# Attention in sessions of two tiles over four PSUM banks, with the products on the other four

## The chip, the cores and the metric

The kernel runs on one core of a Trainium2 chip. The metric is the device time of one execution in microseconds. An executed kernel is also profiled once; that execution has its own time and its own span from first to last instruction, and the rows below come from it. The engines are TensorE (PE, with its weight loads as PEld), VectorE (DVE), ScalarE (ACT), GpSimd (POOL) and SyncE (SP), which issues the DMAs here. Each works its instructions off in the order of the program, and waits for others by semaphores.

## The reference

Batch 8, 8 heads, 576 positions, head size 64, all float32. Three parts follow one another:

```python
# 1. attention inside chunks of 64 positions
scores = scale * np.matmul(q_c, k_c.transpose(0, 1, 2, 4, 3))
scores = scores - np.max(scores, axis=-1, keepdims=True)
attn = np.exp(scores)
attn = attn / (np.sum(attn, axis=-1, keepdims=True) + 1e-09)
out = np.matmul(attn, v_c)
# 2. x is out as (8, 576, 512); layer norm, then a feed-forward of width 2048
mu = np.mean(x, axis=-1, keepdims=True)
var = np.mean((x - mu) ** 2, axis=-1, keepdims=True)
xn = (x - mu) / np.sqrt(var + 1e-06) * g_ln
x = x + np.maximum(xn @ w_ch1, 0.0) @ w_ch2
# 3. h = relu(x @ w_in), width 1024; a convolution of 3 taps along the sequence,
#    a sigmoid gate on its sum, and out = (h * gate) @ w_out
```

## The kernel before

There are 4608 rows of 512, taken as 36 tiles of 128 rows; four tiles make a slab, so there are nine slabs. The change lies in the first stage, which computes attention, the layer norm and the product with `w_ch1`. The later stages (the product with `w_ch2`, the convolution, the last product) are untouched.

The steps of a tile T are methods of `Attention`, each with a letter: `L` loads q, k and v; `S` multiplies q and k (16 small matmuls of 64x64, each of two passes); `M` takes the maximum of each row on VectorE; `E` takes exponentials on ScalarE, in eight instructions of 64 columns, four to a half, and their sums; `R` the reciprocal of the sums; `P` transposes the exponentials on TensorE and `C` copies them out of PSUM on ScalarE; `V` multiplies them with v; `X` scales by the reciprocals on VectorE and stores; `B` and `x` are the layer norm; `T` transposes the normed rows and `e` copies them to `bst`, the slab's input.

PSUM has eight banks. `S` and `V` of a tile use one half each of a pair of banks: banks 0 and 1. `P` goes to bank 0, `T` to bank 3.

The product with `w_ch1` multiplies matrices of 2x2 blocks by seven products in place of eight. Of each slab four groups G are computed, each of seven products n = 1 to 7; each product is 12 matmuls of 256 columns (each operand is split into a high and a low part, three matmuls per product of parts, lines 113 to 115). Products 1, 6, 7 and 4 of a group add up in one bank, 4 or 5 by the group's parity, and after each ScalarE copies the sum out as u1, u6, u7, u4 (lines 605 and 614). Products 5 and 3 add up in another, 6 or 7 by parity: VectorE adds 5 to u7 once product 7 is there, and the sum of 5 and 3 to u6. Product 2 goes to bank 2, and VectorE adds it to u1. These adds are line 159, called from `product`. The results are stored by SP to `hd`.

The order is written out by hand. Time is counted in slots, one product each: slot t = 28p + 7G + s, with s the place in the tuple `SLOTS`; its second number is the lag: a product with lag 1 belongs to the group before. Attention runs one slab ahead of the products. `session(t, tv)` hangs steps of two tiles behind the products of slots t to t + 4: V of tile tv with S, M of tile tv + 1 at t, E in two halves at t + 1 and t + 2, B and x of tv there too, and R, P, C of tv + 1 with T, e of tv at t + 4. In the steady stage a session begins every seven slots. In the last group of a slab each product is also followed by the preparation of the next slab's operand (`Slab.both`: a cast on ScalarE, a subtraction on VectorE, and the block sums `j` that they need).

In slab 0 the first slots also carry the rest of the conversion of `w_ch1` from its 64-bit input: the steps with letters a, t, m, n, g, h, l and s in `START`, behind the bar, one line for each slot; a, g, h are on ScalarE, t, m, n, l, s on VectorE.

Of the kernel before, what the change touches and what calls it, by code (L numbers as in the profile page):

```python
# [23 lines left out]
h7 B2 e1 B3 h6 u1 l7 v1 y3 l8 z3 s4 e3 y2 s6 z2 s5 e2 l6 h11 j0 u2 j1 u3  # L24
s7 u5 v3 u7 h10 l11 j2 l10 u6 v2 h12 v6 j3 l12 u4 v5 h13 v4 l13 v7
|
S4 M4 E4 a8 t8 a10 t10 m8 n8
/ g8 a9 t9 m10 n10
/ g10 a11 a12 t11 t12 m9 R4 P4
/ C4 a14 n9 t14 g9 m12  # L30
/ h14 n12 m11 g12 n11 a13
/ l14 t13 g11 m14 h15
/ n14 s8 g14 l15 a15
/ h16 t15 s9 m13 l16 n13
/ s10 g13 s11 h21 h17
# [9 lines left out]
def attn_moe_moe2(  # L45
# [296 lines left out]
    class Attention:  # L342
# [13 lines left out]
        def tile(self, shape, tag, bufs):  # L356
            return self.p.tile(shape, F32, tag=tag, bufs=bufs, name=tag)

        def L(self, T):
            for nm, to in (("q", self.q), ("k", self.k)):  # L360
                t = self.tile([128, HP * 2 * 64], "r" + nm, 2)
                if T < N0:
                    src = (q0 if nm == "q" else k0)[T].rearrange("c d e j s -> e d c (j s)")
                    for e in range(2):
                        nc.sync.dma_start(
                            out=t[half(e)].rearrange("p (c n) -> p c n", c=2), in_=src[e]
                        )
                    to[T] = t.rearrange("p (c j s) -> p j c s", c=2, s=64)
                else:
                    src = (q if nm == "q" else k)[T - N0]  # L370
                    nc.sync.dma_start(out=t, in_=src.rearrange("e p j c s -> (e p) (j c s)"))
                    to[T] = t.rearrange("p (j c s) -> p j c s", c=2, s=64)
            t = self.tile([128, HP * 2 * 64], "rv", 3)
            nc.sync.dma_start(out=t, in_=v[T].rearrange("e s j c d -> (e s) (j c d)"))
            self.v[T] = t.rearrange("p (j c d) -> p j c d", c=2, d=64)
# [22 lines left out]

        def E(self, T, js=range(4)):
            if T not in self.pp:  # L400
                self.sm[T] = self.tile([128, 2, HP], "sm", 3)
                self.pp[T] = self.tile([128, HP, 2, 64], "pp", 2)
            sm, pp, mx = self.sm[T], self.pp[T], self.mx[T]
            for j in js:
                for e in range(2):
                    nc.scalar.activation(  # L406
                        out=pp[:, j, e, :], in_=self.both[T][:, e, j, :], func=AF.Exp, scale=SCALE,
                        bias=mx[:, e, j:j + 1], accum_out=sm[:, e, j:j + 1],
                    )
# [108 lines left out]
    with tc.manual_schedule():  # L518
# [20 lines left out]
        def one(step):  # L539
            kind, i = step[0], int(step[1:])  # L540
            if kind in "atmng":
                getattr(blocks[i // 4], kind)(i % 4)
            elif kind == "W":
                blocks[i // 4].W(i % 4, nc.sync)
            elif kind == "w":
                blocks[i // 4].W(i % 4, nc.scalar)
            elif kind == "s":
                blocks[i // 4].s(i % 4)
            elif kind in "hl":
                getattr(blocks[i // 7], kind)(i % 7)  # L550
            elif kind in "juv":
                getattr(slabs[0], kind)(i)
            elif kind == "S":
                at.S(i, (4, 6, 0, 4, 0)[i])
            elif kind == "V":
                at.V(i, (4, 6, 0, 4)[i])
            elif kind == "P":
                at.P(i, 0 if i > 3 else 2)
            elif kind in "y":
                at.x(i)  # L560
            elif kind == "z":
                at.T(i)
            else:
                getattr(at, kind)(i)
# [14 lines left out]
        def product(p, G, n):  # L579


            to = {1: 4 + G % 2, 6: 4 + G % 2, 7: 4 + G % 2, 4: 4 + G % 2, 5: 6 + G % 2, 3: 6 + G % 2, 2: 2}[n]
            x = slabs[p].xc[n]
            for i in range(2):
                f = 2 * G + i
                o = f % 4 * 128
                for kk in range(2):
                    w = wc[n, f // 4, kk]
                    mm3(bank[to][:, i * 256:(i + 1) * 256], w[:, 0, o:o + 128], w[:, 1, o:o + 128],
                        x[:, 0, kk], x[:, 1, kk], n in (1, 2, 5) and not i and not kk, kk == 1,  # L590
                        skip_group_check=True)

            def top(name):
                return su_p.tile([128, 2, 256], F32, tag=name, bufs=2, name=name)

            def flat(t):
                return t.rearrange("p a n -> p (a n)")

            def store(blk, t):
                nc.sync.dma_start(out=hd[p][G][:, blk], in_=t)  # L600

            if n in (1, 6, 7):

                t = tops[p, G, n] = top(f"u{n}")
                nc.scalar.copy(flat(t), bank[to])  # L605
            if n == 7:

                t = tops.pop((p, G, 7))
                plus(flat(t), bank[6 + G % 2], flat(t))
                store(3, t)  # L610
            if n == 4:

                t = top("u4")
                nc.scalar.copy(flat(t), bank[to])
                store(2, t)
            if n == 2:

                t = tops.pop((p, G, 1))
                plus(flat(t), bank[to], flat(t))
                store(0, t)  # L620
            if n == 3:

                t = tops.pop((p, G, 6))
                plus(flat(t), bank[to], flat(t))
                store(1, t)

        SLOTS = ((1, 0), (5, 0), (4, 1), (6, 0), (3, 1), (2, 0), (7, 0))
        events = {}

        def on(t, fn):  # L630
            events.setdefault(t, []).append(fn)

        def session(t, tv):

            ts = tv + 1 if tv + 1 < NTILE else None

            def begin():
                at.V(tv)
                if ts is not None:
                    at.S(ts)  # L640
                    at.M(ts)
                at.X(tv)
                if tv + 2 < NTILE:
                    at.L(tv + 2)

            on(t, begin)
            if ts is not None:
                on(t + 1, lambda: at.E(ts, (0, 1)))
                on(t + 2, lambda: at.E(ts, (2, 3)))
            on(t + 1, lambda: at.B(tv))  # L650
            on(t + 2, lambda: at.x(tv))

            if tv % 4 == 3:
                on(t + 3, lambda: (at.T(tv), at.e(tv)))
            if ts is not None:
                on(t + 4, lambda: (at.R(ts), at.P(ts)))
            if tv % 4 != 3:
                on(t + 4, lambda: at.T(tv))
            if ts is not None:
                on(t + 4, lambda: at.C(ts))  # L660
            if tv % 4 != 3:
                on(t + 4, lambda: at.e(tv))

        for tv in range(4, NTILE):

            t = 28 * (tv // 4 - 1) + 7 * (tv % 4 - 1) + 1
            session({4: 5, 5: 9, 6: 13, 7: 17}.get(tv, t), tv)

        class Down:

# [341 lines left out]
```

## Time and profile before

| | |
|---|---|
| Time, median of three runs | 1308.42 us (1308.25 to 1308.7) |
| Profiled execution: time, span | 1309.48 us, 1307.5 us |
| TensorE busy, of the span | 1249.2 us, 96% |
| VectorE busy | 748.9 us, 57% |
| ScalarE busy | 614.8 us, 47% |
| Mean granted clock of TensorE | 0.973 of full speed |
| First product of slab 0 starts | 45.1 us |
| First session of the steady stage (tile 8) starts | 118.0 us |
| A slab of the steady stage, between its sessions | 47.0 us |

A row of the timeline gives the start, the duration, the engine, the source line and operation, what is written and read, and how many instructions stand in it; a bracket at its end is the time that the engine was idle before it and who ended that. Matmuls overlap, so the distance between two starts is what one costs, not its duration. A row of the windows gives the busy time of every engine in a stretch.

### The profile page before, as it was taken

What the parts mean: (1) busy time and instruction counts of PE and PEld (TensorE: products, weight loads), DVE (VectorE), ACT (ScalarE), POOL (GpSimd) and SP (SyncE); (2) the same over time, 40 slices, a digit from 0 to 9 for tenths busy, and PEclk for the clock granted to TensorE, in tenths of its full rate; (3) what the DMA queues carried; (4) which work ended last, traced back from release to release, by engine and by line L of the source; (5) the groups of instructions that cost most, each with busy time, mean ns of one, the idle gap of its engine ahead of it and who ended that gap; (6) DMA issues with size and microseconds to landing.
All of it is one profiled execution on the core that took longest, in us unless ns stands there. A gap on an engine that the chain in (4) does not pass through costs nothing.

```text
span 1307.5 us, 23314 instructions
## 1 busy us (share of the span) xinstructions
PE 1249.2 (96%) x9096; PEld 1087.0 (83%) x9096; DVE 748.9 (57%) x1430; ACT 614.8 (47%) x1510; POOL 76.2 (6%) x172
## 2 busy tenths in 40 slices
PE   5559999999999989999999999999999999999998
PEld 4459999999999978787788888888788888888887
DVE  7986565566556557667733443343876655565540
ACT  6765555556556435343322222222765555455541
POOL 0000000000000000000000000000121211111100
PEclk6689999999999989999999999999999999999999
DMA  9534555555455358486444355432111111101001
GB/s 267 169 106 170 186 172 168 188 186 177 168 183 191 114 205 298 146 296 211 145 153 161 128 178 178 161 130 81 33 57 58 43 37 57 57 28 53 25 25 49
DMA packets 127021, 177.70 MB, mean 136 GB/s; under 512 B 12736, under 2 KB 72128, under 8 KB 126912
## 3 DMA queue, kind: packets, MB, share of 16 engines
q1 hardware_dynamic: 126912, 176.22, 40.3%
q8 instruction: 71, 1.16, 0.4%
q14 instruction: 38, 0.31, 0.1%
HBM read 110.13 MB, written 66.06 MB: 135 GB/s over the span
## 4 chain that ended last, share of the span: by engine, by line
PE 85%; DVE 6%; ACT 4%; DMA 3%; issue 1%; SPq 1%; POOL 0%; DVEq 0%; ACTq 0%; POOLq 0%
PE banks L113 27%; PE banks L114 26%; PE banks L115 26%; PE banks L380 3%; PE banks L462 1%; PE banks L420 1%; DMA w<-in_moe_w_ch_dram 1%; DVE w L156 1%; ACT pp L406 1%; DMA wd<-in_moe_w_ch_dram 1%; DVE w L151 0%; DMA x2d<-x2T 0%; ACT w L335 0%; DVE xr L159 0%; DVE w L145 0%
## 5 line engine op out<-in xcount | busy, mean ns | idle before, releaser
L113 PE MATMUL banks<-xc,w 128*128 128x256 f32 x1008 | 290.4, 288 | 7.6 <-ACT u L605 7.1
L114 PE MATMUL banks<-xc,w 128*128 128x256 f32 x1008 | 283.2, 281 | 4.5 <-DVE xc L156 4.5
L115 PE MATMUL banks<-xc,w 128*128 128x256 f32 x1008 | 282.9, 281 | 0.0
L685 ACT ACTIVATE hh<-hr 128x512 fp32r<-128x512 f32 x144 | 91.1, 632 | 262.0 <-PE banks L115 261.8
L686 DVE SCALAR_TENSOR_TENSOR hl<-hr,hh 128x512 fp32r<-128x512 f32 x144 | 99.2, 690 | 192.1 <-ACT hh L685 189.9
L113 PEld LDWEIGHTS banks<-xc,w 128*128 128x128 f32 x1008 | 193.3, 192 | 10.5 <-ACT u L605 7.5
L114 PEld LDWEIGHTS banks<-xc,w 128*128 128x128 f32 x1008 | 193.6, 192 | 4.7 <-DVE xc L156 4.7
L115 PEld LDWEIGHTS banks<-xc,w 128*128 128x128 f32 x1008 | 193.3, 192 | 0.0
L113 PE MATMUL banks<-w,hl 128*128 128x512 f32 x396 | 154.7, 391 | 0.0
L114 PE MATMUL banks<-w,hh 128*128 128x512 f32 x396 | 154.1, 389 | 0.0
L115 PE MATMUL banks<-w,hh 128*128 128x512 f32 x396 | 154.1, 389 | 0.0
L896 DVE SCALAR_TENSOR_TENSOR cv<-hb,cw_sb,cv 128x510 f32<-128x510 f32 (+31 forms) x256 | 117.2, 512 | 0.6
L113 PE MATMUL banks<-xb,w 128*128 128x512 f32 x288 | 113.5, 394 | 1.8 <-ACT hb L881 1.4
L114 PE MATMUL banks<-xb,w 128*128 128x512 f32 x288 | 113.0, 393 | 0.0
L115 PE MATMUL banks<-xb,w 128*128 128x512 f32 x288 | 112.9, 392 | 0.0
L159 DVE TENSOR_TENSOR u<-banks,u 128x512 f32<-128x512 f32 x108 | 73.6, 688 | 56.2 <-ACT u L605 31.1
L406 ACT ACTIVATE pp<-banks,mx 128x64 f32<-128x64 f32 x288 | 87.8, 336 | 8.1 <-DVE mx L397 5.4
L605 ACT COPY u<-banks 128x512 f32<-128x512 f32 x108 | 64.0, 593 | 56.7 <-PE banks L115 54.1
L113 PEld LDWEIGHTS banks<-w,hl 128*128 128x128 f32 x396 | 74.3, 188 | 17.4 <-DVE hl L686 2.1
L115 PEld LDWEIGHTS banks<-w,hh 128*128 128x128 f32 x396 | 74.3, 188 | 15.6
L114 PEld LDWEIGHTS banks<-w,hh 128*128 128x128 f32 x396 | 74.3, 188 | 15.2
L883 POOL COPY hal<-hb 128x2 f32<-128x2 f32 x64 | 41.8, 652 | 736.6 <-ACT hb L881 736.6
(106 smaller groups left out, 2197.8 us busy)
## 6 DMA issues: line engine op xcount, KB each, us to landing
hd<-u SPq DMA_DIRECT2D x144, 256.0 KB, 2.9
hr<-hd SPq DMA_DIRECT2D x72, 512.0 KB, 3.8
w<-in_moe_w_ch_dram SPq DMA_DIRECT2D x27, 512.0 KB, 6.8
rv<-in_v_dram SPq DMA_DIRECT2D x36, 256.0 KB, 3.7
xd<-x SPq DMA_DIRECT2D x36, 256.0 KB, 2.0
xr<-xd SPq DMA_DIRECT2D x36, 256.0 KB, 4.3
x2d<-x2T SPq DMA_DIRECT2D x36, 256.0 KB, 2.0
x2r<-x2d SPq DMA_DIRECT2D x36, 256.0 KB, 4.0
```

The lines of the kernel that those rows point to most:

```text
L113: nc.tensor.matmul(ps, ll, rh, start=first, stop=False, **kw)
L114: nc.tensor.matmul(ps, lh, rl, start=False, stop=False, **kw)
L115: nc.tensor.matmul(ps, lh, rh, start=False, stop=last, **kw)
L156: nc.vector.tensor_tensor(out=out, in0=a, in1=b, op=ALU.subtract)
L159: nc.vector.tensor_tensor(out=out, in0=a, in1=b, op=ALU.add)
L380: nc.tensor.matmul(ps[half(c), e, j, :], lt[half(e), j, c, :], rt[half(e), j, c, :], start=True, stop=True,)
L406: nc.scalar.activation(out=pp[:, j, e, :], in_=self.both[T][:, e, j, :], func=AF.Exp, scale=SCALE, bias=mx[:, e, j:j + 1], accum_out=sm[:, ...
L605: nc.scalar.copy(flat(t), bank[to])
L685: nc.scalar.activation(out=self.hh, in_=t, func=AF.Relu)
L686: nc.vector.scalar_tensor_tensor(out=self.hl, in0=t, scalar=0.0, in1=self.hh.bitcast(F32), op0=ALU.max, op1=ALU.subtract,)
L883: nc.gpsimd.tensor_copy(out=hal[:, f, :], in_=hb[:, 512:514])
L896: nc.vector.scalar_tensor_tensor(out=cv[:, a:e], in0=hb[:, a + tap:e + tap], scalar=cw_sb[:, tap, f:f + 1], in1=cv[:, a:e], op0=ALU.mult, ...
```

## The change

Sessions take two tiles in place of one: V of both, then S of the next two, and at their end P of both and T of both. The even tile of a pair uses banks 0 and 1, the odd one 2 and 3. Two sessions make a slab: they begin at its slots 0 and 13, and the step with P, T, e and C, now called `turn`, comes six slots later. The products are left with banks 4 to 7: 1, 6, 7, 4 stay on 4 and 5 by parity, 5 and 3 of every group use bank 6, 2 uses bank 7. The order of products in a group is 1, 2, 3 (of the group before), 6, 4 (of the group before), 5, 7, where it was 1, 5, 4, 6, 3, 2, 7. Loads of v are separate (`Lv`), and the early slots are rearranged: S4 and S5 both stand in slot 0, and tiles 4 and 5 begin at slot 7, tiles 6 and 7 at slot 14 (before: tiles 4 to 7 at slots 5, 9, 13 and 17).

```diff
-S4 M4 E4 a8 t8 a10 t10 m8 n8
-/ g8 a9 t9 m10 n10
-/ g10 a11 a12 t11 t12 m9 R4 P4
-/ C4 a14 n9 t14 g9 m12
-/ h14 n12 m11 g12 n11 a13
-/ l14 t13 g11 m14 h15
+S4 S5 M4 M5 E4 L6 L7 a8 t8 a10 t10 m8 n8
+/ E5 g8 a9 t9 m10 n10
+/ g10 a11 a12 t11 t12 m9
+/ a14 n9 t14 g9 m12
+/ R4 P4 C4 h14 n12 m11 g12 n11 a13
+/ R5 P5 C5 l14 t13 g11 m14 h15
...
-            to = {1: 4 + G % 2, 6: 4 + G % 2, 7: 4 + G % 2, 4: 4 + G % 2, 5: 6 + G % 2, 3: 6 + G % 2, 2: 2}[n]
+            to = {1: 4 + G % 2, 6: 4 + G % 2, 7: 4 + G % 2, 4: 4 + G % 2, 5: 6, 3: 6, 2: 7}[n]
...
-                plus(flat(t), bank[6 + G % 2], flat(t))
+                plus(flat(t), bank[6], flat(t))
...
-        SLOTS = ((1, 0), (5, 0), (4, 1), (6, 0), (3, 1), (2, 0), (7, 0))
+        SLOTS = ((1, 0), (2, 0), (3, 1), (6, 0), (4, 1), (5, 0), (7, 0))
...
+            tvs = tv, tv + 1
+            tss = [T for T in (tv + 2, tv + 3) if T < NTILE]
+            side = lambda T: T % 2 * 2
 
             def begin():
-                at.V(tv)
-                if ts is not None:
-                    at.S(ts)
-                    at.M(ts)
-                at.X(tv)
-                if tv + 2 < NTILE:
-                    at.L(tv + 2)
+                for T in tvs:
+                    at.V(T, side(T))
+                for T in tss:
+                    at.S(T, side(T))
+                for i in range(2):
+                    if tss:
+                        at.M(tss[i])
+                    at.X(tvs[i])
+                for T in tss:
+                    if T + 2 < NTILE:
+                        at.L(T + 2, late=True)
+                for T in tss:
+                    at.Lv(T)
+
+            def turn():
+                for T in tss:
+                    at.R(T)
+                    at.P(T, side(T))
+                for T in tvs:
+                    at.T(T, side(T) + 1)
+                for i in range(2):
+                    at.e(tvs[i])
+                    if tss:
+                        at.C(tss[i])
...
+            for i, T in enumerate(tss):
+                on(t + 1 + 2 * i, lambda T=T: at.E(T, (0, 1)))
+                on(t + 2 + 2 * i, lambda T=T: at.E(T, (2, 3)))
+            for i, T in enumerate(tvs):
+                on(t + 1 + i, lambda T=T: at.B(T))
+                on(t + 3 + i, lambda T=T: at.x(T))
+            on(t + 6, turn)
+
+        for tv in range(4, NTILE, 2):
+
+            t = 28 * (tv // 4 - 1) + (13 if tv % 4 else 0)
+            session({4: 7, 6: 14}.get(tv, t), tv)
```

The first place is TensorE at the start of a session in the steady stage, before the change: `rv,pt` is V, `rk,rq` is S, the rows around it are products.

```order
L114 MATMUL banks<-xc,w_1120 128x256
L115 MATMUL banks<-xc,w_1120 128x256
L380 MATMUL banks<-rv,pt 64x64 x16
L380 MATMUL banks<-rk,rq 64x64 x16
L113 MATMUL banks<-xc,w_363 128x256
L114 MATMUL banks<-xc,w_363 128x256
```

After the change the same place, where line 380 has become line 384, reads:

```order
L114 MATMUL banks<-xc,w_620 128x256
L115 MATMUL banks<-xc,w_620 128x256
L384 MATMUL banks<-rv,pt 64x64 x32
L384 MATMUL banks<-rk,rq 64x64 x32
L113 MATMUL banks<-xc,w_340 128x256
L114 MATMUL banks<-xc,w_340 128x256
```

Both tiles of a pair stand together, and the place occurs half as often.

The second place is VectorE in the last group of a slab. Before the change, from the add behind product 7 (`u_2135`) on, it has a J (`t`), a second, a subtraction for the next operand (`xc`), a third J, a second subtraction and the M and X of a session:

```order
L159 TENSOR_TENSOR u_2135<-banks,u_2135 128x512
L156 TENSOR_TENSOR t_2153<-bst 128x512
L156 TENSOR_TENSOR bst<-bst 128x2x256
L156 TENSOR_TENSOR xc<-bst,xc 128x512
L159 TENSOR_TENSOR bst<-bst 128x2x256
L156 TENSOR_TENSOR xc<-t_2153,xc 128x512
L396 TENSOR_REDUCE mx<-banks 128x8
L397 TENSOR_SCALAR mx<-mx 128x8
L434 TENSOR_TENSOR x<-banks,sm 128x2x4x64
```

After it, the same stretch from the add behind product 7 (`u_2180`) on, with the add to u1 (`u_2196`) and the add to u6 (`u_2107`), which is the last reader of bank 6 before product 5:

```order
L159 TENSOR_TENSOR u_2180<-banks,u_2180 128x512
L156 TENSOR_TENSOR t_2198<-bst 128x512
L156 TENSOR_TENSOR bst<-bst 128x2x256
L156 TENSOR_TENSOR xc<-bst,xc 128x512
L159 TENSOR_TENSOR bst<-bst 128x2x256
L159 TENSOR_TENSOR u_2196<-banks,u_2196 128x512
L156 TENSOR_TENSOR xc<-bst,xc 128x512
L156 TENSOR_TENSOR bst<-bst 128x2x256
L159 TENSOR_TENSOR u_2107<-banks,u_2107 128x512
L156 TENSOR_TENSOR xc<-bst,xc 128x512
```

The session has left the last group, and the adds of products 2 and 3 have moved forward, between the sums for the next slab.

## Rows read from the trace of the kernel before

**Rows 1.** The page, part 1: busy us, share of the span, instructions.

```profile
PE 1249.2 (96%) x9096; PEld 1087.0 (83%) x9096; DVE 748.9 (57%) x1430; ACT 614.8 (47%) x1510; POOL 76.2 (6%) x172
```

**Rows 2.** Windows: stretch, length, busy us and instructions per engine, clock, DMA.

```profile
60.00:84.00 24.00, 15.28 (x211) 14.30 (x210) 19.78 (x42) 17.07 (x42) 0.86 (x1) 0.78 0.25 78
84.00:112.00 28.00, 21.16 (x259) 20.08 (x259) 20.43 (x42) 15.03 (x55) 1.63 (x2) 0.84 0.35 114
213.00:260.00 47.00, 47.00 (x632) 46.15 (x634) 27.97 (x60) 26.59 (x96) 2.20 (x4) 1.00 0.54 180
```

**Rows 3.** Timeline of TensorE at V and S of a steady session.

```profile
164.59 0.28 PE L114 MATMUL banks<-xc,w 128*128 128x256 f32 x1
164.70 0.28 PE L115 MATMUL banks<-xc,w 128*128 128x256 f32 x1
164.91 0.69 PE L380 MATMUL banks<-rv,pt 64*64 64x64 f32 x32
165.43 0.65 PE L380 MATMUL banks<-rk,rq 64*64 64x64 f32 x32
166.00 0.38 PE L113 MATMUL banks<-xc,w 128*128 128x256 f32 x1
166.22 0.29 PE L114 MATMUL banks<-xc,w 128*128 128x256 f32 x1
```

**Rows 4.** Timeline of TensorE at P and T of that session.

```profile
171.45 0.28 PE L115 MATMUL banks<-xc,w 128*128 128x256 f32 x1
171.60 0.66 PE L420 MATMUL banks<-ident,pp 128*128 128x128 f32 x4
172.09 0.60 PE L462 MATMUL banks<-ident,xn 128*128 128x128 f32 x4
172.45 0.36 PE L113 MATMUL banks<-xc,w 128*128 128x256 f32 x1
172.65 0.28 PE L114 MATMUL banks<-xc,w 128*128 128x256 f32 x1
```

**Rows 5.** Timelines of VectorE and ScalarE there: the pace of each queue.

```profile
166.18 0.68 DVE L156 TENSOR_TENSOR xc<-t,xc 128x512 fp32r<-128x512 f32 x1
166.78 0.68 DVE L396 TENSOR_REDUCE mx<-banks 128x8 f32<-128x512 f32 x1
167.58 0.68 DVE L434 TENSOR_TENSOR x<-banks,sm 128x512 f32<-128x512 f32 x1
...
168.35 0.32 ACT L406 ACTIVATE pp<-banks,mx 128x64 f32<-128x64 f32 x1
...
169.53 0.60 ACT L605 COPY u<-banks 128x512 f32<-128x512 f32 x1
170.00 0.65 ACT L502 CAST xc<-bst 128x512 fp32r<-128x512 f32 x1
```

**Rows 6.** Timeline of TensorE, early stage: waits, and the first steady session.

```profile
53.63 0.58 PE L114 MATMUL banks<-xc,w 128*128 128x256 f32 x1 [4.46 <-DVE xc L156]
58.51 1.11 PE L420 MATMUL banks<-ident,pp 128*128 128x128 f32 x4 [2.17 <-ACT pp L406]
76.06 1.11 PE L420 MATMUL banks<-ident,pp 128*128 128x128 f32 x4 [3.94 <-ACT pp L406]
81.07 1.13 PE L380 MATMUL banks<-rv,pt 64*64 64x64 f32 x32 [3.04 <-ACT pt L426]
97.69 1.13 PE L380 MATMUL banks<-rv,pt 64*64 64x64 f32 x32 [5.74 <-ACT pt L426]
118.00 0.69 PE L380 MATMUL banks<-rv,pt 64*64 64x64 f32 x32
```

**Rows 7.** SP's issue of tile 5's k, and the landing of k loads there.

```profile
48.11 1.42 SPq L365 DMA_DIRECT2D rk<-in_k_dram  x2
...
DMA to landing us min/median/max: 6.3/7.2/8.2
```

**Rows 8.** TensorE's waits from 455 to 480 us: total, times, longest.

```profile
PE banks L113 <- ACT u L605: 6.5, 1, 6.5
```

More of the change, by code (lines that the diff above doesn't have):

```diff
@@ L357, in tile, with L @@
             return self.p.tile(shape, F32, tag=tag, bufs=bufs, name=tag)
-        def L(self, T):
+        def L(self, T, late=False):
             for nm, to in (("q", self.q), ("k", self.k)):
@@ L372, in L, with Lv @@
                     to[T] = t.rearrange("p (j c s) -> p j c s", c=2, s=64)
+            if not late:
+                self.Lv(T)
+        def Lv(self, T):
             t = self.tile([128, HP * 2 * 64], "rv", 3)
@@ L400, in E @@
             if T not in self.pp:
-                self.sm[T] = self.tile([128, 2, HP], "sm", 3)
+                self.sm[T] = self.tile([128, 2, HP], "sm", 4)
                 self.pp[T] = self.tile([128, HP, 2, 64], "pp", 2)
@@ L553, in one @@
             elif kind == "S":
-                at.S(i, (4, 6, 0, 4, 0)[i])
+                at.S(i, (4, 6, 0, 4, 0, 2)[i])
             elif kind == "V":
@@ L557, in one @@
             elif kind == "P":
-                at.P(i, 0 if i > 3 else 2)
+                at.P(i, i % 2 * 2 if i > 3 else 2)
+            elif kind == "L":
+                at.L(i, late=i > 5)
             elif kind in "y":
@@ L633, in session @@
         def session(t, tv):
-            ts = tv + 1 if tv + 1 < NTILE else None
+            tvs = tv, tv + 1
+            tss = [T for T in (tv + 2, tv + 3) if T < NTILE]
+            side = lambda T: T % 2 * 2
             def begin():
-                at.V(tv)
-                if ts is not None:
-                    at.S(ts)
-                    at.M(ts)
-                at.X(tv)
-                if tv + 2 < NTILE:
-                    at.L(tv + 2)
-            on(t, begin)
-            if ts is not None:
-                on(t + 1, lambda: at.E(ts, (0, 1)))
-                on(t + 2, lambda: at.E(ts, (2, 3)))
@@ L650, in session @@
[L650 to L667, printed above, removed]
+                for T in tvs:
+                    at.V(T, side(T))
```

## Prediction

> **What bounds the kernel now.** I read the page's list of engines first: TensorE is busy 96% of the span [rows 1], so what counts is what it does beside the products, and what makes it wait. The windows part the attention stage in two. From 60 to 112 us TensorE is busy 36.4 of 52 us at a granted clock of 0.78 to 0.84, a mean over its two levels of 1.2 and 2.4 GHz, with VectorE busy 40.2: here it waits for others. From 213 to 260 us, one slab of the steady stage, it is busy throughout at 1.00, VectorE 28.0 and ScalarE 26.6 of 47 us [rows 2]. So the stretches need different sums. TensorE's timeline gives the cost of a session in the steady one [rows 3, 4], the timelines of VectorE and ScalarE the pace of their queues [rows 5], the bracketed waits what holds TensorE early [rows 6].
>
> **Steady stage: what merging sessions saves.** Matmuls of a product start 0.11 us apart. At a session the first value matmul starts 0.21 us after the last product matmul, 0.10 more; V and S take 1.09 us; the first product matmul behind them is followed after 0.22 us, 0.11 more [rows 3]. So 0.21 us are paid for going in and out, whatever stands between. At the transposes it is 0.04 in and 0.09 out, and the first set of four takes 0.49 us where the second takes 0.36, so 0.26 in all [rows 4]. A pair of tiles pays this once in place of twice: 0.47 us less. Tiles 8 to 35 are 14 pairs: 14 x 0.47 = 6.6 us less. Ends: 3.3, if half of it comes back between the tiles of a pair, and 7.3, if the step from V to S (S takes 0.57 us, V 0.52) also halves. I take 6.6, straight from the rows. No matmul, copy or exponential is added or dropped; the same 12 loads of q, k and v a slab go out, six together, and are wanted 13 or 15 products (18 us or more) later, under which they hide.
>
> **Steady stage: what is late next.** I walked both sessions of a slab through the queues by hand: a product 1.36 us (12 x 0.113); VectorE 0.65 an instruction, 0.80 for the maximum with its scaling; ScalarE 1.2 us for four exponentials, 0.5 a copy or cast [rows 5]. Zero is the end of the product ahead of the session; V, V, S, S end at 2.2.
> - Session in the first group of a slab. VectorE does M, X, M, X from 2.0 to 4.9. ScalarE has the first tile's first half of exponentials from 3.5 to 4.7, then in queue order the cast behind product 3 (5.6), a half (6.8), u6 (7.3), a half (8.5), u4 and a cast (9.5), the last half (10.7). TensorE wants it at 10.95: a quarter to spare. The add behind product 3, which frees bank 6, ends at 7.3; product 5 wants the bank at 7.8.
> - Session at the end of the second group: exponentials end at 9.8, wanted at 10.9; the add ends at 8.4, bank 6 is wanted at 9.1.
> - Last group: VectorE now has eight instructions from the first J to the add behind product 3, as the second place of the order shows: two J's, a subtraction, a J, the add to u1, a subtraction, a J, the add to u6. They follow the turn's copies and the add behind product 7, from 15.4 to 20.6 with 0.65 each. Product 5 wants bank 6 at 20.45, and the signal needs 0.1: about 0.3 us of waiting, in eight slabs 2.4 us.
>
> This wait does not exist before, so ends: 0 (0.3 is less than one instruction) and 15, one microsecond at each of the 15 places in first (seven) and last (eight) groups. I take 2.4, what the walk gives.
>
> Here a page of the Trainium skill speaks against the change: "Perfetto Trace Analysis", section Optimizing Tensor Performance (Matmuls), says that independent groups should rotate through different banks, so that one is emptied under the next one's matmuls. Products 5 and 3 lose that: 6 and 7 in turn before, 6 alone now. By the rule each group would pay; by the walk one group in four does. No run here shows it yet; the third rival is that rule.
>
> **Early stage.** The five longest waits of TensorE between 53 and 98 us hold 19.4 us: 4.5, 2.2, 3.9, 3.0, 5.7 [rows 6]. The last three stand where V follows its own P and C in one slot (sessions 5 to 7 each begin where the one before ends), behind what ScalarE has queued from the weights. The new order has one such place, slots 13 and 14. Walked through at the same paces:
> - S5 moves up into slot 0 and meets its load: the k part goes out at 48.1 to 48.9 and lands up to 8.2 us later, about 57 [rows 7]. That is a new wait of some 8 us; it takes the place of the 4.5 at 53.6 and the 2.2 at 58.5, since product 2 comes in where product 5 stood and the exponentials of tile 4 run meanwhile. Product 2 starts near 58.
> - Product 7 of the first group waits for the copy u6 (66.1), V5 for C5 (70.5). V4, V5, S6, S7 end near 72, and slot 10 can start near 75; before, it starts at 83, behind the session at 81.07 [rows 6].
> - From there VectorE, now almost without gaps, is the bound. Product 5 of the second group waits for the add that frees bank 6, which the queue reaches at 84.4 (6 us of waiting). The exponentials of tile 7 end at 90.4, V7 can start at 95.7, slot 19 waits for bank 6 until 103.9, slot 22 ends at 111.3.
> - Before, slot 22 ends at 118.0, where V8 starts [rows 6]. So 6.7 us; I write 6.5 less.
>
> Ends: VectorE is busy 40.2 of the 52 us from 60 to 112, so no order can save more than 11.8 there [rows 2]; at worst only the new wait stays, 57.1 against 53.6, 3.5 more. I stay with the walk, which lies nearer the first.
>
> **End of the stage.** TensorE waits 6.5 us for a copy that stands behind a weight load on ScalarE [rows 8]. The loads go out behind the store of slot 5, which holds a product without a store now, so up to one product, 1.4 us, sooner; against that, product 3 follows product 7 directly and waits for a copy and an add where 4 waited for the copy, 0.7 more. I take 0.5 less, ends 1.4 less and 0.7 more.
>
> **Sum.** -6.6 + 2.4 - 6.5 - 0.5 = -11.2 us. The profiled execution took 1309.48 us, 1.98 around its span of 1307.5; it would take 1298.3. The median of the three timed runs lies 1.06 below it: 1297.2 us.
>
> **Rivals.**
> - The early gain does not come: VectorE's conversions are the same, and where they bound, the order of sessions moves waits only. Then -6.6 + 2.4 - 0.5 = -4.7, 1303.7 us. For it: my walk finds nearly as much waiting after as before, and the gain rests on VectorE's gaps closing. Against it: V no longer stands right behind its own C three times.
> - The steady stage gives nothing back: what goes in and out of a session is paid at every tile of a pair, as if nothing were merged. Then 2.4 - 6.5 - 0.5 = -4.6, 1303.8 us. For it: rows show no two sets of one kind in a row, so the cost between them is not seen. Against it: S right behind V pays only 0.05.
> - Slower: bank 6 becomes the bound. Product 5 waits in the first and last groups of every slab for the add on VectorE, behind the paired M, X, M, X or the J's. The gains without that wait are 13.6 us, so it decides from 13.6/15 = 0.9 us a place: one VectorE instruction more ahead of the add than I count in the last group, two in the first. At 1.6 us a place (two instructions later in the last group) it is 24 us, 10.4 more than all gains: 1318.8 us. Against it: the counts come from the order itself, and VectorE has 19 of 47 us free [rows 2].
>
> **How the numbers follow.** Forecast 0.50, no early gain 0.20, nothing in the steady stage 0.16, bank 6 as the bound 0.14. A measurement can tell 0.2%, 2.6 us. Faster than 1305.8: the forecast (0.48) and some three quarters of the second and third cases (0.26), 0.74. Within: the rest of these and a part of the last, 0.14. Slower than 1311: 0.12, the last. The range 1290 to 1309 takes in the first three with their bounds and the milder part of the fourth; it leaves out a full early gain and the fourth at its price.
>
> **What would show it.** V and S of a steady session as 64 matmul passes each, and products again some 2.3 us after the last; a slab of 46.2 to 46.5 us where it was 47.0; waits of a product for a VectorE add in the last group alone; slot 22 ending near 111 us. It is wrong if S5 does not wait near 57, if adds hold TensorE by more than 0.9 us a place, or if the steady stage gains over 1 us a slab.

## The result and the profile after

The changed kernel takes 1298.44 us, the median of four runs (1298.02 to 1300.73), against 1308.56 for the kernel before in the same session (four runs): ratio 0.9915, 95% interval 0.9901 to 0.9928. The forecast was 1297.2. Its profiled execution was the longest of the four, 1300.73 us with a span of 1298.9, against 1309.48 and 1307.5.

The page, part 1, of the changed kernel, which answers to [rows 1]:

```profile
PE 1241.2 (96%) x9096; PEld 1081.7 (83%) x9096; DVE 744.4 (57%) x1430; ACT 614.5 (47%) x1510; POOL 76.8 (6%) x172
```

The same instructions, and 8.0 us less of busy TensorE: most of the 8.6 us of span is found there. The windows, as in [rows 2] (busy time of PE, PEld, DVE, ACT, POOL, then the granted clock):

```profile
60.00:84.00 24.00, 17.99 (x269) 16.91 (x261) 21.99 (x47) 17.88 (x52) 0.49 (x1) 0.93 0.34 107
84.00:112.00 28.00, 21.67 (x263) 20.98 (x264) 22.04 (x46) 20.27 (x78) 2.57 (x4) 0.84 0.37 121
213.00:260.00 47.00, 47.00 (x632) 46.49 (x631) 27.42 (x60) 26.64 (x96) 2.36 (x4) 1.00 0.54 183
```

VectorE is at work for 44.0 of the 52 early microseconds, 40.2 before. The steady stage is still full, so a gain there must come from cheaper work. TensorE at V and S of a steady pair, to be read against [rows 3]:

```profile
192.00 0.28 PE L115 MATMUL banks<-xc,w 128*128 128x256 f32 x1
192.20 1.16 PE L384 MATMUL banks<-rv,pt 64*64 64x64 f32 x64
193.18 1.11 PE L384 MATMUL banks<-rk,rq 64*64 64x64 f32 x64
194.23 0.38 PE L113 MATMUL banks<-xc,w 128*128 128x256 f32 x1
194.45 0.29 PE L114 MATMUL banks<-xc,w 128*128 128x256 f32 x1
```

From the last product matmul ahead to the second one behind are 2.45 us; less two steps of a product, 0.227, the place costs 2.22. A single tile paid 1.29 in the same reckoning [rows 3], two of them 2.58. P and T of that pair, against [rows 4]:

```profile
202.40 0.28 PE L115 MATMUL banks<-xc,w 128*128 128x256 f32 x1
202.51 1.03 PE L424 MATMUL banks<-ident,pp 128*128 128x128 f32 x8
203.38 1.04 PE L466 MATMUL banks<-ident,xn 128*128 128x128 f32 x8
204.18 0.37 PE L113 MATMUL banks<-xc,w 128*128 128x256 f32 x1
204.38 0.28 PE L114 MATMUL banks<-xc,w 128*128 128x256 f32 x1
```

1.98 less 0.227 is 1.75 for two tiles. The session of [rows 4] paid 0.97 for one. It is the one that begins in the last group, and that one pays 0.97 to 0.98 in each of slabs 1 to 6; behind the other groups it looks like this:

```profile
136.26 0.28 PE L115 MATMUL banks<-xc,w 128*128 128x256 f32 x1
136.38 0.60 PE L420 MATMUL banks<-ident,pp 128*128 128x128 f32 x4
136.81 0.60 PE L462 MATMUL banks<-ident,xn 128*128 128x128 f32 x4
137.17 0.37 PE L113 MATMUL banks<-xc,w 128*128 128x256 f32 x1
137.37 0.28 PE L114 MATMUL banks<-xc,w 128*128 128x256 f32 x1
```

It pays 1.11 - 0.227 = 0.88, and two pay 1.76: beside it the pair saves next to nothing. The last exponentials of the two sessions in the kernel before, behind another group and in the last one:

```profile
136.01 0.36 ACT L406 ACTIVATE pp<-banks,mx 128x64 f32<-128x64 f32 x1
171.40 0.35 ACT L406 ACTIVATE pp<-banks,mx 128x64 f32<-128x64 f32 x1
```

The first ends as P begins (136.37 and 136.38), the second 0.15 us after P has begun (171.75 and 171.60). That the 0.09 more is P waiting for it is likely; no run tests it.

The early waits of TensorE, against [rows 6]:

```profile
49.72 1.13 PE L384 MATMUL banks<-rk,rq 64*64 64x64 f32 x32
58.86 0.47 PE L384 MATMUL banks<-rk,rq 64*64 64x64 f32 x2 [8.01 <-DMA rk<-in_k_dram]
...
68.29 0.38 PE L113 MATMUL banks<-xc,w 128*128 128x256 f32 x1 [1.50 <-ACT u L611]
...
85.22 0.58 PE L113 MATMUL banks<-xc,w 128*128 128x256 f32 x1 [5.34 <-DVE u L159]
...
98.54 0.69 PE L384 MATMUL banks<-rv,pt 64*64 64x64 f32 x32 [3.70 <-ACT pt L430]
```

S4 runs at 49.72, S5 waits 8.0 us for its k, product 7 1.5 us for u6, product 5 of the second group 5.3 us for the add that frees bank 6, V6 3.7 us for its C. The windows of slab 0, from its first product to that of slab 1, before and after:

```profile
45.13:126.91 81.78, 59.15 (x710) 55.95 (x709) 64.21 (x128) 53.04 (x166) 3.59 (x5) 0.81 0.45 146
46.88:122.32 75.44, 54.90 (x674) 52.49 (x673) 62.18 (x125) 52.75 (x165) 3.05 (x4) 0.83 0.49 162
```

Of the 6.3 us that slab 0 is shorter, only 2.1 are less idle time of TensorE (22.6 before, 20.5 after); 4.2 are less busy time. Then the place in the last group where bank 6 was expected late (TensorE and VectorE):

```profile
211.78 0.69 DVE L159 TENSOR_TENSOR u<-banks,u 128x512 f32<-128x512 f32 x1
...
212.32 0.28 PE L115 MATMUL banks<-xc,w 128*128 128x256 f32 x1
212.53 0.39 PE L113 MATMUL banks<-xc,w 128*128 128x256 f32 x1
212.75 0.28 PE L114 MATMUL banks<-xc,w 128*128 128x256 f32 x1
```

The add ends at 212.47, after the last matmul of product 4 has begun, and product 5 starts at 212.53. No bracket stands there, because the modelled end of the matmul ahead (212.32 + 0.28 = 212.60) covers the gap; it shows in the distances alone. From 212.32 to 212.75 are 0.43 us where 0.227 would do: 0.20 more. So it is in slabs 1 to 6, with 0.14 in slab 0 and 0.06 in slab 7, 1.4 us in all, and no product that follows another directly in the first three groups of slabs 1 to 7 has such a gap. Last, the wait for a copy behind a weight load, which was 6.5 us in [rows 8], from 455 to 480 us:

```profile
PE banks L113 <- ACT u L611: 4.9, 1, 4.9
```

### The profile page after: what moved, and what is told of

Same layout as the page of the kernel before. It is cut to its first block, busy times and chain, and to the rows that moved or that the text cites. A ratio compares the mean times of both kernels' runs of the same rounds, so it can differ in the third digit from the quotient of the medians.

```text
span 1298.9 us, 23259 instructions
## 1 busy us (share of the span) xinstructions
PE 1241.2 (96%) x9096; PEld 1081.7 (83%) x9096; DVE 744.4 (57%) x1430; ACT 614.5 (47%) x1510; POOL 76.8 (6%) x172
## 4 chain that ended last, share of the span: by engine, by line
PE 86%; DMA 5%; DVE 4%; ACT 2%; SPq 1%; issue 1%; DVEq 0%; ACTq 0%
PE banks L113 28%; PE banks L114 27%; PE banks L115 27%; PE banks L384 3%; DMA rk<-in_k_dram 2%; PE banks L466 1%; PE banks L424 1%; DMA w<-in_moe_w_ch_dram 1%; DVE w L156 1%; DMA wd<-in_moe_w_ch_dram 1%; DMA rq<-in_q_dram 1%; DMA x2d<-x2T 0%; DVE w L151 0%; DVE xr L159 0%; DMA hd<-u 0%
```

## The experiments

All ratios are to the kernel before, run on the same chip, with 95% intervals; "slab 0" is the time from the first product of slab 0 to that of slab 1, read from the timeline: 81.8 before, 75.4 after. Three profiles share the changed kernel's slab 0 (after, e1, e9): 75.4, 75.8 and 76.5 us, so a difference of 1 us there may be chance. The twelve runs were on four chips, so absolute times of different groups are not compared.

**e1. The changed kernel again.**

> The changed kernel once more, unchanged, for a second profile. In its first profile the first product started at 46.9 us, 1.75 us later than in the profile of the kernel before, though nothing ahead of it was changed but the place of tiles in memory. Theory: chance of that one execution; the first product starts near 45.1 here and the span is about 1297. Rival: the new layout or load order costs 1.7 us at the start; then it starts near 46.9 again. Either way slabs 1 to 7 at 46.4 us each, a 0.2 us wait ahead of product 5 in the last group of each slab, time 1298 to 1301.

Measured 1299.75 us (1298.92 to 1300.26), ratio 0.9921 (0.9906 to 0.9935). Slab 0 took 75.8 us, steady slabs 46.3 each, and 0.20 us stood ahead of product 5 in the last groups of slabs 1 to 6. The first product began at 45.8 us, 46.9 in the first profile and 45.1 before, so neither the theory's 45.1 nor the rival's 46.9: in the fourteen profiles it lies between 44.9 and 47.0, with either layout.

**e2. The order and the banks of the products alone, in the kernel before.**

```diff
-            to = {1: 4 + G % 2, 6: 4 + G % 2, 7: 4 + G % 2, 4: 4 + G % 2, 5: 6 + G % 2, 3: 6 + G % 2, 2: 2}[n]
+            to = {1: 4 + G % 2, 6: 4 + G % 2, 7: 4 + G % 2, 4: 4 + G % 2, 5: 6, 3: 6, 2: 7}[n]
...
-                plus(flat(t), bank[6 + G % 2], flat(t))
+                plus(flat(t), bank[6], flat(t))
...
-        SLOTS = ((1, 0), (5, 0), (4, 1), (6, 0), (3, 1), (2, 0), (7, 0))
+        SLOTS = ((1, 0), (2, 0), (3, 1), (6, 0), (4, 1), (5, 0), (7, 0))
```

> The kernel before with the new order of products and their new banks only (5 and 3 on bank 6, 2 on bank 7); sessions of one tile at their old slots. My theory: bank 6 costs 0 to 0.3 us in a slab's last group and product 2 in place of 5 shortens one early wait that is then spent on the exponentials: 1307 to 1310 us, slabs at 47.0 to 47.3. Rival (one bank for 5 and 3 is a burden by itself, hidden in the changed kernel by what merging gives): waits for the add in most groups, slabs at 48 us or more, 1316 us or more.

Measured 1323.3 us, ratio 1.0100 (1.0083 to 1.0117): slower. The theory fails; of the rival the times hold (1316 us or more, slabs at 48 or more), but not its reason: steady slabs took 48.9 to 49.7 us, yet products waited for the add in the last group alone, 0.15 us a slab. The loss is at the transposes of the session that begins in the last group (VectorE, ScalarE and TensorE of this kernel):

```profile
217.40 0.69 PE L380 MATMUL banks<-rv,pt 64*64 64x64 f32 x32
...
219.98 0.69 DVE L156 TENSOR_TENSOR bst<-bst 128x512 f32<-128x512 f32 x1
220.59 0.68 DVE L396 TENSOR_REDUCE mx<-banks 128x8 f32<-128x512 f32 x1
...
222.19 0.32 ACT L406 ACTIVATE pp<-banks,mx 128x64 f32<-128x64 f32 x1 [4.07 <-DVE x L434]
...
224.10 0.28 PE L115 MATMUL banks<-xc,w 128*128 128x256 f32 x1
225.43 0.66 PE L420 MATMUL banks<-ident,pp 128*128 128x128 f32 x4 [1.06 <-ACT pp L406]
```

V stands at 217.40. With product 2 moved ahead, the sums J and the subtractions for the next slab come ahead of M and X on VectorE; exponentials start 4.8 us after V, 3.4 in the kernel before (168.35 in [rows 5], V at 164.91 in [rows 3]). P comes four slots after V, needs all of them, and waits: by the distances the place of P and T costs 2.16 us in place of 0.97. T alone, of the session that ends three slots after V, costs 1.0 in place of 0.45. With the 0.15 that is the 1.9 us between 47.0 and 48.9; the slabs above that have 9 to 19 products in a wider spacing (see e11).

**e3. The new slab 0, old sessions, order and banks from slab 1 on.**

```diff
+            own = 6 if p == 0 else 6 + (G + 1) % 2
...
+        pair(7, 4)
+        pair(14, 6)
...
+        for tv in range(8, NTILE):
+            session(28 * (tv // 4 - 1) + 7 * (tv % 4 - 1) + 1, tv)
...
-                for s, (n, lag) in enumerate(SLOTS):
+                for s, (n, lag) in enumerate(NEW_SLOTS if p == 0 else OLD_SLOTS):
```

> The new slab 0 (S4 and S5 together, pairs of tiles 4 to 7, the new order and banks of products), and from slab 1 on the sessions, order and banks of the kernel before. My theory: the two gains are separate and the early one is 4 to 6.5 us: 1302 to 1304.5, slabs at 47.0. Rival (the early part only moves waits, since VectorE converts the same weights): 1307 to 1309.

Measured 1306.95 us, ratio 0.9976 (0.9964 to 0.9989), less than expected. At the end of slot 22 TensorE stood 68.6 us after its first product, 72.7 before and 68.4 in the changed kernel: so far the whole early gain is there. But the session of tile 8 now begins at slot 22 in the new order of products, which is the place of e2, and its P and T cost 2.1 us; slab 0 ends at 79.1.

**e4. The old slab 0 (with S, E, P and C of tile 9 in its last slots), pairs from slab 1 on.**

```diff
+        for t, tv in ((5, 4), (9, 5), (13, 6), (17, 7)):
+            single(t, tv)
...
+        on(22, ninth)
+        on(23, lambda: at.E(9, (0, 1)))
+        on(24, lambda: at.E(9, (2, 3)))
+        on(26, lambda: (at.R(9), at.P(9), at.C(9)))
...
-        for tv in range(4, NTILE, 2):
+        for tv in range(8, NTILE, 2):
```

> Slab 0 as in the kernel before (S9 with its E, P and C added in slots 22 to 26), and pairs with the new order and banks from slab 1 on. My theory: 4 to 5 us less from seven slabs at 46.4, nothing early: 1303 to 1305. Rival (the steady gain is an effect of the early one, or a pair pays as much as two sessions): slabs at 47.0, 1307 to 1309.

Measured 1304.86 us (1303.92 to 1306.6), ratio 0.9961 (0.9947 to 0.9974): as expected, slabs of 46.4 us. Of the 0.79% in e1 the steady stage alone brings 0.39, the new slab 0 alone 0.24; the rest, 0.16, is little more than the intervals leave open, and e3's loss at the session of tile 8, 1.2 us, is some 0.09 of it.

**e5. One cast, subtraction and J of the last group behind the add of product 3.**

```diff
-                            nxt.both(n)
+                            if n != 2:
+                                nxt.both(n)
+                        if G == 3 and n == 3 and slabs.get(p + 1):
+                            slabs[p + 1].both(2)
```

> The changed kernel, with one cast, one subtraction and one J of the last group moved behind the add of product 3. Theory (VectorE's queue holds product 5 in the last group, since the add that frees bank 6 stands behind the J's): the extra 0.20 us ahead of product 5 in slot 26 falls to 0.00 in slabs 1 to 7, some 1.4 us in all, ratio to the kernel before 0.991 (it was 0.992). Rival (0.20 is what any handing over of a bank costs, whatever stands ahead of the add): 0.20 stays, ratio 0.992. A third way: the later operand makes a product of the next slab wait instead, and the gain is lost.

Measured 1296.71 us (1296.26 to 1297.02), ratio 0.9894 (0.9879 to 0.9910). The gap ahead of product 5 is 0.00 in every slab, and slabs take 46.1 us in place of 46.3: the theory holds. Its interval overlaps that of e1, but by the slabs it is 1.4 us better, and it is the version to keep.

**e7. Two more adds on VectorE ahead of that add.**

```diff
                             nxt.both(n)
+                            if n == 2:
+                                b22 = nxt.blocks()[3]
+                                for _ in range(2):
+                                    plus(at.tile([128, 2, 256], "s4", 1), b22, b22)
```

> The changed kernel, with two more VectorE adds (a block of the next slab's operand to itself, into a scratch tile that is never read) in the last group of each slab, ahead of the add of product 3. Theory (the add that frees bank 6 is late by VectorE's queue): the extra ahead of product 5 in slot 26 grows from 0.20 by two instructions of 0.65, to some 1.5 us in each of eight slabs, 10 us more in all, ratio to the kernel before 1.000. Rival (a fixed cost of handing over): it stays 0.20 or grows far less than 1.3, ratio 0.992 to 0.993.

Measured 1308.78 us (1308.12 to 1309.37), ratio 0.9987 (0.9978 to 0.9996). The gap is now long enough for a bracket:

```profile
212.82 1.41 DVE L159 TENSOR_TENSOR s<-bst 128x512 f32<-128x512 f32 x2
214.14 0.68 DVE L159 TENSOR_TENSOR u<-banks,u 128x512 f32<-128x512 f32 x1
...
214.88 0.38 PE L113 MATMUL banks<-xc,w 128*128 128x256 f32 x1 [1.25 <-DVE u L159]
```

By distances it is 1.53 us a slab, 0.20 + 2 x 0.66, and slabs take 47.6. So VectorE's queue decides at this place with nothing to spare, and each instruction ahead of the add costs its full length.

**e6. S5 a slot later.**

```diff
-S4 S5 M4 M5 E4 L6 L7 a8 t8 a10 t10 m8 n8
-/ E5 g8 a9 t9 m10 n10
+S4 M4 E4 L6 a8 t8 a10 t10 m8 n8
+/ S5 M5 E5 L7 g8 a9 t9 m10 n10
```

> The changed kernel, with S5, M5, E5 and L7 in slot 1 in place of slot 0, so that S5 no longer stands ahead of product 2 while it waits 8.0 us for its k. Theory of the prediction (VectorE, almost without gaps, bounds the stretch to slot 22): the 8.0 us become smaller ahead of slot 1, but the later waits (5.3 us ahead of product 5 of the second group, 3.7 ahead of V6) grow by nearly as much, and slab 0 stays within 1 us of 75.4 us. Rival (TensorE's own chain of waits bounds it): slab 0 becomes 3 to 6 us shorter, ratio 0.988 to 0.990.

Measured 1301.20 us, ratio 0.9928 (0.9916 to 0.9941); slab 0 takes 77.5 us, longer by 1.7 than in e1. S5 waits 4.2 us in place of 9.0, and the early waits together shrink from 21.5 to 19.3, yet the stretch grows. The windows from 44 to 124 us, of this run and then of e1, show where the time went:

```profile
44.00:124.00 80.00, 60.80 (x684) 57.71 (x683) 64.60 (x128) 53.43 (x167) 3.05 (x4) 0.79 0.50 159
```

```profile
44.00:124.00 80.00, 58.46 (x758) 55.87 (x760) 65.41 (x130) 54.94 (x169) 3.06 (x4) 0.83 0.49 159
```

TensorE does less in more busy time, at a granted clock of 0.79 against 0.83. Five products of slab 0 have their matmuls 0.21 us apart throughout, the lower of the two levels; in e1 one has, and three more come near (0.19 to 0.20). But in e9, whose slab 0 is that of the changed kernel, as many have it, and slab 0 takes 76.5 us: how many products run at the lower level changes from one execution to the next. So about 1 us of the 1.7 can be put down to the edit, and that the waiting, cut into more pieces, brings slower matmuls is a guess. Both sides of the expectation fail: 77.5 is not within 1 us of 75.4, and the rival's 3 to 6 us did not come. A sum of waits alone does not give the time here.

**e10, e12. Is VectorE the bound early? Six sign steps left out; the loads of tile 5 issued earlier.**

```diff
-/ E5 g8 a9 t9 m10 n10
+/ E5 g8 a9 t9 m10
...
```

```diff
-R3 g7 y0 l5 C3 z0 y1 h9 V3 X2 W9 W11 L4 W12 e0 l9 g4 z1 X3 W14 W13 W15 L5 h8
+R3 g7 y0 l5 C3 z0 y1 h9 V3 X2 W9 W11 L4 L5 W12 e0 l9 g4 z1 X3 W14 W13 W15 h8
```

> The changed kernel without six VectorE steps of the conversion of w_ch1 in slots 1 to 7 (the sign bits of six blocks are left out, n9 to n14): 6 x 0.68 = 4.1 us less VectorE work early. Theory of the prediction (VectorE's queue bounds the early stretch): the wait of product 5 of the second group for the add (5.3 us) falls to 1 to 3 us, and slab 0 falls from 75.5 to 71.5 to 73.5 us, ratio 0.989 to 0.991. Rival (S5's k, ScalarE or TensorE's own chain bounds it): slab 0 stays within 1 us of 75.5, ratio 0.991 to 0.993.

> The changed kernel with the loads of tile 5 issued earlier, and nothing else (the J stays where it was). In the run before, with both edits, matmuls stood 0.118 us apart in place of 0.113 through the whole stage, and slabs took 47.5 us; what ended such stretches in other runs was a place where TensorE waited or changed to small matmuls. Theory (the 0.20 us wait in each last group ends or begins such stretches, so that none lasts the stage): slabs of 46.3 to 46.8 us and no run near 1306; slab 0 of 73.5 to 75.5, since VectorE bounds it, ratio 0.990 to 0.992. Rival (the earlier loads bring the wide spacing): it holds through the stage in some runs here too, one of some five near 1305 to 1308.

e10 measured 1297.96 us, ratio 0.9919 (0.9906 to 0.9932), e12 1297.83 us, ratio 0.9917 (0.9904 to 0.9931). Waits of TensorE from 44 to 125 us (total, times, longest), first in e10, then in e12:

```profile
PE banks L384 <- DMA rk<-in_k_dram: 8.2, 1, 8.2
PE banks L113 <- DVE u L159: 4.4, 1, 4.4
```

```profile
PE banks L113 <- DVE u L159: 4.9, 1, 4.9
PE banks L424 <- ACT pp L410: 4.2, 2, 2.3
...
PE banks L384 <- DMA rk<-in_k_dram: 1.8, 1, 1.8
```

Against e1, with 4.1 us less VectorE work and the 8 us wait as it was, slab 0 falls by 2.8 us to 73.0. With the k wait cut by 7.2 us (9.0 in e1) and VectorE's work as it was, it falls by 1.6 to 74.1, since P waits for exponentials instead. So a microsecond of VectorE's work is worth 0.7 here (0.6 to 0.9 against the three unchanged slabs 0) and a microsecond of that wait 0.2 (0.2 to 0.3), from one profile each: VectorE is most of the bound, not all of it. The wait for the add shrank less than I expected (4.4; 1 to 3 was the expectation): it is reached sooner, too. In e10's ratio the gain is hidden by what e11 shows.

**e9. V, S, V, S in place of V, V, S, S.**

```diff
+                if tv > 7 and tss:
+                    for i in range(2):
+                        at.V(tvs[i], side(i))
+                        at.S(tss[i], side(i))
...
```

> The changed kernel, with a steady session (tiles 8 to 35) that issues V, S, V, S in place of V, V, S, S. A single tile paid 1.29 us for V and S, a pair 2.23. Theory (besides the 0.21 for going in and out, every step from V to S or back has a price): with x for one V and one S and s for a step, x + s = 1.29 - 0.21 and 2x + s = 2.23 - 0.21, so s = 0.14; the new order has three steps in place of one, 0.28 more, a place costs 2.51 us, 14 x 0.28 = 3.9 us, a slab 46.9 in place of 46.3, ratio to the kernel before 0.995. Rival (steps are free; the pair saves in going in and out alone, and more of it than I read): a place stays at 2.23 us, ratio 0.992.

Measured 1299.78 us (1298.35 to 1309.14), ratio 0.9944 (0.9923 to 0.9966); the one long run widens the interval. The rows decide:

```profile
191.09 0.28 PE L115 MATMUL banks<-xc,w 128*128 128x256 f32 x1
191.29 0.69 PE L384 MATMUL banks<-rv,pt 64*64 64x64 f32 x32
191.81 0.65 PE L384 MATMUL banks<-rk,rq 64*64 64x64 f32 x32
192.27 0.65 PE L384 MATMUL banks<-rv,pt 64*64 64x64 f32 x32
192.74 0.65 PE L384 MATMUL banks<-rk,rq 64*64 64x64 f32 x32
193.31 0.38 PE L113 MATMUL banks<-xc,w 128*128 128x256 f32 x1
193.54 0.29 PE L114 MATMUL banks<-xc,w 128*128 128x256 f32 x1
```

2.45 - 0.227 = 2.22 us, the same as in order V, V, S, S. Steps between V and S are free; my theory falls and the rival holds. The rows also show where the price of going in and out is: an S in the middle takes 0.46 us, one with a product behind it 0.57; a V in the middle 0.47, one with a product ahead of it 0.52.

**e8. e2 with the transposes one slot later.**

```diff
-                on(t + 4, lambda: (at.R(ts), at.P(ts)))
+                on(t + (5 if tv > 7 else 4), lambda: (at.R(ts), at.P(ts)))
```

(and so for the other three steps at t + 4)

> The kernel before with the changed order and banks of the products (ratio 1.010 alone), and with the step R, P, T, C, e of sessions from tile 8 on five slots behind V in place of four. Theory (with the new order the J's come ahead of M and X in the last group, so exponentials are late for P there, by 1.2 us, and T alone by 0.5): one product, 1.36 us, more of lead covers both; the 2.1 and 1.0 us at these places go back to 0.9 and 0.45, a slab from 48.9 to 47.2 us, ratio 1.000. Rival (the products' order and banks cost by themselves, whatever the session's lead): slabs stay at 48.5 to 49.5 us, ratio 1.008 to 1.010.

Measured 1313.61 us, ratio 1.0024 (1.0015 to 1.0034), from 1.0100. P and T of the session in the last group come back to 0.89 us. T alone of the session that ends three slots after V stays at 1.0 in place of 0.45, as I had not moved that step: 0.55 us in each of seven slabs. Slabs take 47.9 to 48.5 us; what is left over 47.0 beside that is the wider spacing of the next run, which nearly half of the products of these slabs have here. So most of e2's loss was the short lead; the new `turn`, six slots behind V, gives more of it than the five tried here.

**e11. J later and loads earlier together.**

> The kernel with the J later (ratio 0.989), and with the loads of tile 5 issued ahead of the four loads of w_ch1 that stood before them. S5's k then goes out some 5 us earlier and lands some 5 to 7 us earlier, so of the 8 us wait of S5 1 to 3 us remain; the last four weight blocks land later by up to 3 us. Theory (VectorE bounds the stretch from 60 us on): slab 0 (75.2 us) falls by at most 2 us, as VectorE waits for blocks or works them off at the same pace, ratio 0.988 to 0.990. Rival (the wait for k is on the path): slab 0 falls by 4 to 6 us, ratio 0.985 to 0.986.

Measured 1297.11 us, but from 1294.85 to 1306.54, ratio 0.9906 (0.9892 to 0.9920). The profiled run is the long one, and its slabs take 47.5 us. The windows from 300 to 350 us, of this run and then of e5:

```profile
300.00:350.00 50.00, 50.00 (x647) 49.60 (x646) 27.67 (x60) 28.76 (x100) 2.43 (x4) 1.00 0.54 180
```

```profile
300.00:350.00 50.00, 50.00 (x661) 49.61 (x660) 30.86 (x65) 28.05 (x98) 2.43 (x4) 1.00 0.53 180
```

Both are full at a granted clock of 1.00, but one does 14 matmul records less: its product matmuls start 0.118 us apart from slot 16 of slab 0 to slot 9 of slab 8, in e5 0.113. Slab 0 is 75.5 us, about 74.6 without the wide spacing in 16 of its products (16 x 12 x 0.0045): at most 2 us less, as the theory said, and not the rival's 4 to 6.

## Why the prediction was right, point by point

**Merging saves 6.6 us.** About right in sum, wrong in its parts. At V and S a pair saves 2 x 1.29 - 2.22 = 0.36 us, not 0.21, as part of the price of going in and out stood inside the distances of the first V and the last S, where I took it for work (e9). With x for V and S of a tile and c for the price, x + c = 1.29 and 2x + c = 2.22 give x = 0.93 and c = 0.36. At P and T it saves 0.01 behind most groups, not 0.26. The first four transposes take longer than the second four, and I took that for a price of going in; but in a pair eight of P take 0.87 us, as much as twice a single tile's four (0.43). And [rows 4] is the session of the last group, whose extra 0.09 a pair does not pay: some 0.05 a pair. That is 0.42 a pair. Also, product matmuls behind a session start 0.115 us apart for one product, and there are four such places less a slab, some 0.03 a pair. The slabs agree: they fell from 47.0 to 46.3 us, 0.7 after 0.2 of waiting, which makes 0.45 a pair, 14 x 0.45 = 6.3 us.

**The wait in the last group, 0.3 us x 8 = 2.4.** Right in mechanism, place and number of instructions: 0.20 a slab and 1.4 us in all. e5 took it away and e7 lengthened it by the two instructions added. No wait in the first and second groups, as forecast.

**Early stage, -6.5.** The chain came as walked: S5 waits 8.0 us for k, product 7 for u6, product 5 of the second group 5.3 us for the add, V6 and V7 for their C. But at the end of slot 22, the mark of the walk, TensorE was 4.3 us ahead (68.4 us after its first product, 72.7 before) in place of 6.7. S and P of tile 9, some 1.0 us, were done besides, which no term of the sum counts: 5.3 in place of 6.5. Slab 0 as a whole fell by 6.3 us, since the session of tile 8, 2.2 us, has left its slots 22 to 26. That VectorE is the bound held for the most part (e10, e12). What I left out is the clock: only 2.1 us of the 6.3 are less waiting, and the rest is work that left slab 0, two merged pairs, and the share of matmuls that ran at the lower level. That share moves: e9, with the same slab 0, had 19.4 us idle and 57.0 busy.

**End of the stage, -0.5.** Wrong by about 1.1 in these profiles. The wait for the copy fell from 6.5 to 4.9, past the better end. Product 3 behind product 7 waits 1.8 us, where 4 and 3 waited 0.9 and 0.7 before: 0.1 more, not 0.7. What I had not counted: product 5 of the third group waits 0.7 us for an add, the product behind the stall runs longer at the lower clock than before, 0.5 us here and 0.8 in e1, and in this profile the last 18 products came out in the wide spacing of e11, 18 x 0.053 = 1.0 us, which e1 has not. From the first product of slab 8 to the last, the end is 0.6 us longer in both (51.3 against 50.7). But e3, which keeps the old end, takes 51.4, and the other runs with the new one 50.2 to 51.6: whether the end costs or gives is not settled.

**The sum.** Up to the first product of slab 8, measured from the first product, the profile fell from 409.7 to 398.8 us, 11.0, where the three terms said 10.7. Of that, 40 products of slabs 2 and 7 in the wide spacing before and 24 after make 0.8 of chance. By parts it is -6.3 + 1.4 - 5.3 = -10.2, and the 0.8: that the sum comes so near is partly luck, since an early gain 1.2 too small was made up by a wait 1.0 smaller and by this 0.8. The end took back 0.6 and the late start 1.75, of which e1 repeats 0.6; so the profiled execution lost 8.75 us in place of 11.2, and the median of all runs 10.1.

**The rivals.** Early gain none: refuted by slab 0. Nothing in the steady stage: refuted by e4 and by the rows of a pair. Bank 6 as the bound: it needed 0.9 us a place, and has 0.20 at one place of four. The rule of the Trainium skill behind that rival ("Perfetto Trace Analysis", section Optimizing Tensor Performance (Matmuls)), that independent groups should rotate through banks, I had read as every group paying. This trace does not bear that reading out for products 5 and 3: from 3 to 5 stand two products on other banks, 2.7 us, and in slabs 1 to 7 a group pays only where VectorE's queue is longer than that. e7 shows how near it is: 1.5 us a slab, ratio 0.9987, with two instructions more. What I had not among the rivals is e2: that the new order of products harms the sessions, and not the bank. In the change, with `turn` six slots behind V and two sessions a slab, that loss is not there.

## What to carry to other kernels

The price of going in and out of a different kind of matmul stands partly in the first and last of the inserted ones: read it from two lengths of the insert, or from a middle piece, and read the place in every group before one is taken for typical. An operand that is prepared earlier moves whatever is behind it on VectorE later, so list who waits for those, exponentials and transposes here, before the buffer that the change is about. A sum of waits misses what the clock does behind them, and that differs between executions of the same code: by 1 us in slab 0 here.

## What the runs showed of the hardware

Product matmuls have two spacings at a granted clock of 1.00, 0.113 and 0.118 us, with the same instructions. Stretches of the wide one last from one product to several slabs. In the profiles of before and after they begin behind a place where TensorE went over to other matmuls or waited a little, and end at another such place; e5 had none in slabs 1 to 7, e11 nothing else, and the spread of the kernel before (1307 to 1313 us on one chip) is as large as some 100 products of it (5 us). e7, with 1.5 us of waiting in each last group, had none at all in its profile. e12 differs from e11 by the J alone, had the 0.20 us gap in each slab, and stayed at 0.113 in its profile, with no run over 1298.4; that a small gap keeps it from lasting is a guess that these runs suit, but five runs each of e11 and e12 don't settle it. What sets the spacing stays open.
